# First V load in three pieces, score tiles in another order, and the third batch's projection moved forward, in a fused linear-attention and FFN kernel

## The chip, the cores and the metric

The kernel runs on one core of one Trainium2 chip. The metric is the device time of one execution in microseconds (us). The kernel before takes 512.08 us (median of three runs, 511.97 to 513.61). A ratio is the mean time of one kernel's runs over the mean of the other's of the same rounds on the same chip, so it is not quite the ratio of the medians that are quoted. Below 1 means faster than the kernel before. "Same" is a difference under 2%.

Engine names in the profile: PE is TensorE, DVE is VectorE, ACT is ScalarE, POOL is GpSimd, SP is SyncE. A "q" after the name (SPq) is the engine's instruction queue, here issuing a DMA.

## The reference

Eight batches of eight heads, 1,024 tokens of 64 features. Keys and values are projected from 1,024 tokens to 64 rows, so attention is against 64 projected keys; its result is the input of a two-layer FFN with squared ReLU.

```python
# q, k, v: (8, 8, 1024, 64); E, F: (64, 1024); w_in: (512, 2048); w_out: (2048, 512)
k_proj = np.einsum('ks,bhsd->bhkd', E, k)
v_proj = np.einsum('ks,bhsd->bhkd', F, v)
scores = scale * np.matmul(q, k_proj.transpose(0, 1, 3, 2))
attn = softmax(scores)                                    # cut: max, exp, sum
x = np.matmul(attn, v_proj)                               # cut: to (8192, 512)
h = np.maximum(x @ w_in, 0.0)
return h * h @ w_out                                      # float32 (8192, 512)
```

## The kernel before

TensorE's order is written by hand; the instructions of the other engines and of the DMA queues are ordered by a scheduler when the kernel is built. The FFN of batch b is the backbone. A plan inserts the attention work of batch b+1, and the projections of batch b+2, between numbered steps of that FFN. In what follows, "second batch" is b = 1, "third batch" is b = 2, and so on.

```python
    qkv_pool = ctx.enter_context(tc.tile_pool(name="qkv", bufs=2))   # two K, two V, two Q tiles, 1 MB each
    out_pool = ctx.enter_context(tc.tile_pool(name="outp", bufs=4))  # o_sb: four tiles of 256 KB
    fps = ctx.enter_context(tc.tile_pool(name="fps", bufs=4, space=bass.MemoryType.PSUM))   # "bank"
    # ... cut ...
    def load(t, src):
        return nc.gpsimd.dma_start(t, src)               # all loads: GpSimd's queue

    def load_kvq(b):
        tiles = []
        for name, src in (("K_sb", k), ("V_sb", v), ("Q_sb", q)):
            t = qkv_pool.tile([P, H, NI, D], BF16, name=name)
            tiles.append((t, load(t[:], tokens(src, b))))
        return tiles
    # ... cut: first K, Q loads in halves ...
    for g in range(2):
        load(V0[:, half[g]], tokens(v, 0, h=half[g]))
    # ... cut ...
    W_IN_PIECES = ((0, 2), (2, 4), (4, 8), (8, 12), (12, 16))
    # ... cut: one load a piece, then four w_out loads, the first batch's second Q half before the last ...

    SCORE_QUADS = ((LO, 0, 0, LO), (HI, 0, 1, LO), (LO, 1, 1, HI), (HI, 1, 0, HI))
    VALUE_QUADS = ((LO, 0, 0, LO), (HI, 0, 1, HI), (HI, 1, 1, LO), (LO, 1, 0, HI))

        def transpose_q_dma(self):                       # SyncE's queue: 1 MB, SBUF to SBUF
            nc.sync.dma_start_transpose(
                self.qT[:].rearrange("p h n t -> p (h n) t"), self.Q[:].rearrange("p h i d -> p (h i d)")
            )

        def scores_mm(self, ps, pr, n):                  # four 64x64 tiles of the array
            for o, par, a, r in SCORE_QUADS:
                h = 2 * pr + a
                nc.tensor.matmul(
                    ps[o, par], lhsT=self.kT[r, h % 4, h // 4, :], rhs=self.qT[r, h, n, :], start=True, stop=True
                )
    # ... cut ...
        def store(self, c, tb, ps, m=slice(0, DM)):      # PSUM -> o_sb by ScalarE, then SyncE's queue
            o = out_pool.tile([P, DM], F32, name="o_sb")
            nc.scalar.copy(o[:, m], ps[:, m])
            i = 2 * (2 * c + tb % 2) + tb // 2
            nc.sync.dma_start(out_rows[self.b, i, :, m], o[:, m])
    # ... cut: the plan of batch b ...
                if b + 2 < B:
                    if b == 0:
                        at(61, coming.project)           # reads the third batch's K and V
                        at(63, coming.transpose_q_dma)
                        at(64, coming.transpose_k)
                    else:
                        at(27, coming.project)
                        at(30, coming.transpose_q_dma)
                        at(29, coming.transpose_k_dma)
```

SyncE's queue carries both the 1 MB transposes of Q and the output stores. And a load into a K, V or Q tile can be issued only when the tile's earlier content has been consumed: K and V by the projection on TensorE, Q by its DMA transpose (from the third batch on).

Names in the profile lines: kp and vp are the projected K and V, kT and qT the transposed kp and Q, xT the attention result, hsq the squared hidden layer of the FFN. ps_bank and ps_att are tiles in PSUM, into which the matmuls write; a "bank" is one of the four ps_bank tiles. o_sb is an output tile in SBUF on its way to memory.

The softmax here doesn't subtract the row's maximum and nothing guards it: scores larger than these inputs give would overflow.

## Time and profile before

| quantity | value | view |
|---|---|---|
| time | 512.08 us (511.97 to 513.61) | runs |
| span in the profile | 510.0 us | page |
| TensorE busy | 497.0 us, 97% | page, part 1 |
| TensorE's longest wait for data | 1.4 us, second half of the first V | waits |
| granted clock | 1.000 | cores |
| FFN period of one batch, later batches | 60.43 to 60.49 us | chain |

The page of the kernel before. In part 2 each column is a fortieth of the span (12.75 us) and a digit is the busy share in tenths; PEclk is the granted TensorE clock. The last line is from part 4, the chain of work that ended last, by engine.

```profile
span 510.0 us, 6889 instructions
...
PE 497.0 (97%) x2710; PEld 222.8 (44%) x2761; DVE 216.7 (42%) x437; ACT 272.4 (53%) x411; POOL 32.0 (6%) x44
...
PE   8799999999999999999999999999999999999997
...
PEclk9999999999999999999999999999999999999999
DMA  9999999899996199104931060101102011010102
...
PE 88%; DMA 7%; issue 2%; POOL 1%; ACT 1%; DVE 1%; POOLq 0%; ACTq 0%
```

TensorE bounds this kernel: it is at 9 in every column but the first two and the last. DMA is at 8 or 9 in the first 12 columns, some 150 us. So the early transfers compete with one another, although TensorE's work hides nearly all of it.

From the waits of TensorE in the kernel before (what waited and for what, us in total, times, longest), the ones that the first V and the last weights cause:

```profile
PE ps_bank L204 <- DMA V_sb<-in_v_dram: 1.4, 1, 1.4
...
PE ps_att L266 <- DVE vp L208: 0.5, 1, 0.5
...
PE ps_bank L364 <- DMA w_out_131<-in_moe_w_out_dram: 0.2, 1, 0.2
```

The first two, 1.9 us, are the second V half and the copy of its projection: they are what the first part of the change addresses.

Now the stretch between 90 and 140 us. First the timeline of GpSimd's queue in the kernel before: start, duration of the issue, engine, line, what is loaded, count, and in brackets the idle time before and what ended it.

```profile
91.02 1.75 POOL L76 DMA_DIRECT2D Q_sb<-in_q_dram  x2 [30.16 <-DMA qT<-Q_sb]
111.09 0.87 POOL L76 DMA_DIRECT2D Q_sb<-in_q_dram  x1 [18.32 <-DMA qT<-Q_sb]
111.95 0.88 POOL L76 DMA_DIRECT2D K_sb<-in_k_dram  x1
112.82 1.09 POOL L76 DMA_DIRECT2D V_sb<-in_v_dram  x1
```

The two loads at 91.02 are Q of the fourth and fifth batch. The one at 111.09 is Q of the sixth batch: it waited 18.3 us for a DMA transpose to consume the tile. The fifth batch's K and V stand behind it in the queue and are issued at 111.95 and 112.82, though their tiles had been free since the third batch's projection, which ended at 87.6 in TensorE's timeline, 24 us earlier.

The timeline of SyncE's queue in the kernel before. The long durations are those of DMA transposes: the queue goes on to the next instruction only when more than half of the transpose has been moved (numbers below).

```profile
101.59 6.96 SPq L248 DMA_TRANSPOSE qT<-Q_sb  x1
108.60 5.32 SPq L373 DMA_DIRECT2D out_dram<-o_sb  x6
116.13 21.16 SPq L248 DMA_TRANSPOSE qT<-Q_sb  x1
```

The transpose issued at 101.59 (Q of the fourth batch) holds the queue for 6.96 us; at 108.60 six output stores follow, the first four of them issued one right after the other by 110.24. The o_sb tiles of these four had been filled at 77.06 to 90.37 (ScalarE's copies): their stores stand behind this transpose in the queue's order, and it waits for its Q, which landed at 101.52. The trace says more. At the end of such an issue, 675, 672 and 669 KB of the 1,049 KB had been started in the first three transposes. The three later ones, which begin with no load beside them, hold the queue 4.0 to 4.2 us and let it go at 800, 852 and 594 KB. While 1 KB load packets run beside it, a transpose (256 B packets) moves 39 KB per us and the loads 154; alone it moves 290. Both kinds have about 152 packets in each us, one for one. The Trainium skill ("DMA: Bandwidth & Descriptors", Queues, rings and completion order) says that each DMA engine takes its queue rows in turn, a packet from each; the equal counts of this trace agree with that. (A packet of that page holds several descriptors; whether a packet record of the trace is one of those is not shown.)

The first of the four stores landed at 111.10. What waits for it, in ScalarE's timeline and then in TensorE's, of the kernel before:

```profile
111.17 0.58 ACT L371 COPY o_sb<-ps_bank 128x512 f32<-128x512 f32 x1 [1.12 <-DMA out_dram<-o_sb]
```

```profile
112.78 1.03 PE L364 MATMUL ps_bank<-w_out_124,hsq 128*128 128x512 bf16 x4
```

ScalarE's copy of an output tile to o_sb starts at 111.17, just after the store that freed that o_sb tile; the matmul group of 112.78 writes the PSUM bank which that copy freed. TensorE did not wait; the slack is about 1 us.

The next transpose, issued at 116.13, holds the queue for 21.16 us, to 137.29. Only two output tiles are copied meanwhile (ScalarE at 118.94 and 122.39), so two of the four o_sb tiles stay free, and TensorE waits for nothing there.

### The profile page before, as it was taken

The page shows a single profiled execution, that of the slowest core. Times are in us where ns is not written, and L with a number is a line of the kernel's source. Part 1 is how long each engine was busy: PE and PEld are TensorE (multiplying, and loading weights), DVE is VectorE, ACT ScalarE, POOL GpSimd, SP SyncE. Part 2 cuts the span into 40 slices and gives each one's busy share as a digit, 9 for nine tenths or more (in the row PEclk, how much of TensorE's full clock was granted, in tenths as well). Part 3 has the DMA queues.
Part 4 walks back from the last instruction along what each step waited for, and adds up shares of the span by engine and source line. Part 5 has one row for each costly group of instructions (what it writes and reads, how often), then busy time and mean ns, then how long its engine had stood idle before and what let it go on. Part 6 is the DMA issues. An engine that isn't in the chain of part 4 may idle for free.

```text
span 510.0 us, 6889 instructions
## 1 busy us (share of the span) xinstructions
PE 497.0 (97%) x2710; PEld 222.8 (44%) x2761; DVE 216.7 (42%) x437; ACT 272.4 (53%) x411; POOL 32.0 (6%) x44
## 2 busy tenths in 40 slices
PE   8799999999999999999999999999999999999997
PEld 4344444444444444444444444444444444444444
DVE  2442766444434445235452345444443443522130
ACT  2564484664718556374645736366472755544351
POOL 7320100121000020001000000000000000000000
PEclk9999999999999999999999999999999999999999
DMA  9999999899996199104931060101102011010102
GB/s 156 204 205 222 226 207 202 132 220 207 195 217 125 56 185 201 65 0 126 181 78 42 17 160 1 62 22 42 53 1 82 1 41 42 31 54 21 63 0 82
DMA packets 67840, 53.92 MB, mean 106 GB/s; under 512 B 29152, under 2 KB 59616, under 8 KB 67808
## 3 DMA queue, kind: packets, MB, share of 16 engines
q0 software_dynamic: 30880, 29.49, 36.8%
q1 hardware_dynamic: 36928, 23.99, 17.5%
q8 instruction: 21, 0.34, 0.3%
q14 instruction: 11, 0.09, 0.1%
HBM read 59.24 MB, written 16.78 MB: 149 GB/s over the span
## 4 chain that ended last, share of the span: by engine, by line
PE 88%; DMA 7%; issue 2%; POOL 1%; ACT 1%; DVE 1%; POOLq 0%; ACTq 0%
PE ps_bank L364 41%; PE ps_bank L358 40%; DMA w_out_131<-in_moe_w_out_dram 4%; DMA w_in_116<-in_moe_w_in_dram 3%; PE ps_bank L185 2%; PE ps_att L256 1%; PE ps_att L290 1%; PE ps_att L312 1%; PE ps_bank L312 1%; DVE rs L300 0%; PE ps_bank L241 0%; DVE xT L341 0%; POOL K_sb L76 0%; POOL V_sb L76 0%; ACT expT L270 0%
## 5 line engine op out<-in xcount | busy, mean ns | idle before, releaser
L355 DVE TENSOR_TENSOR hsq<-h_relu 128x512 bf16<-128x512 bf16 x256 | 108.9, 426 | 192.9 <-ACT h_relu L354 192.0
L354 ACT ACTIVATE h_relu<-ps_bank 128x512 bf16<-128x512 f32 x256 | 151.7, 599 | 69.3 <-PE ps_bank L358 69.2
L364 PEld LDWEIGHTS <-hsq 128*128 128x128 bf16 x1040 | 99.5, 98 | 123.6 <-issue 9.3
L371 ACT COPY o_sb<-ps_bank 128x512 f32<-128x512 f32 (+1 forms) x65 | 37.6, 579 | 119.7 <-PE ps_bank L364 110.9
L364 PE MATMUL ps_bank<-w_out_124,hsq 128*128 128x512 bf16 (+1 forms) x257 | 65.6, 376 | 0.2
L364 PE MATMUL ps_bank<-w_out_131,hsq 128*128 128x512 bf16 (+1 forms) x251 | 64.1, 376 | 1.4 <-issue 1.1
L364 PE MATMUL ps_bank<-w_out_128,hsq 128*128 128x512 bf16 (+1 forms) x252 | 64.3, 376 | 1.1 <-issue 1.0
L364 PE MATMUL ps_bank<-w_out_126,hsq 128*128 128x512 bf16 (+1 forms) x249 | 64.2, 376 | 1.1 <-issue 0.8
L300 DVE COPY rs<-rs 32x1024 f32<-32x1024 f32 x60 | 41.3, 689 | 47.2 <-ACT rs L295 45.8
L358 PE MATMUL ps_bank<-xT,w_in_122 128*128 128x512 bf16 x255 | 58.9, 380 | 0.0
L358 PE MATMUL ps_bank<-xT,w_in_118 128*128 128x512 bf16 x250 | 57.7, 380 | 0.4
L358 PE MATMUL ps_bank<-xT,w_in_120 128*128 128x512 bf16 x247 | 57.4, 379 | 0.4
L270 ACT ACTIVATE expT<-ps_att 128x1024 bf16<-128x1024 f32 x32 | 31.8, 1024 | 18.1 <-PE ps_att L256 18.1
L358 PEld LDWEIGHTS <-w_in_120 128*128 128x128 bf16 x256 | 24.9, 98 | 30.4 <-issue 0.4
L358 PEld LDWEIGHTS <-w_in_118 128*128 128x128 bf16 x256 | 24.9, 98 | 30.2 <-issue 0.4
L358 PEld LDWEIGHTS <-w_in_122 128*128 128x128 bf16 x256 | 24.4, 98 | 31.1 <-issue 2.7
L358 PE MATMUL ps_bank<-xT,w_in_114 128*128 128x512 bf16 x128 | 30.6, 379 | 0.3 <-DVE xT L341 0.2
L358 PE MATMUL ps_bank<-xT,w_in_116 128*128 128x512 bf16 x126 | 30.0, 379 | 0.1
L294 ACT ACTIVATE rs<-ps_att 128x1024 f32<-128x1024 f32 x15 | 15.3, 1023 | 12.7 <-PE ps_att L290 12.7
L316 DVE TENSOR_TENSOR xT<-ps_att,rs 128x512 bf16<-128x512 f32 x28 | 18.1, 686 | 8.7 <-PE ps_att L312 8.4
L358 PEld LDWEIGHTS <-w_in_114 128*128 128x128 bf16 x128 | 12.4, 98 | 15.6 <-issue 1.3
L358 PEld LDWEIGHTS <-w_in_116 128*128 128x128 bf16 x128 | 12.5, 98 | 15.2 <-issue 0.2
(71 smaller groups left out, 233.9 us busy)
## 6 DMA issues: line engine op xcount, KB each, us to landing
out_dram<-o_sb SPq DMA_DIRECT2D x63, 256.0 KB, 2.0
K_sb<-in_k_dram POOLq DMA_DIRECT2D x7, 1024.0 KB, 22.1
V_sb<-in_v_dram POOLq DMA_DIRECT2D x7, 1024.0 KB, 26.7
Q_sb<-in_q_dram POOLq DMA_DIRECT2D x7, 1024.0 KB, 15.0
K_sb<-in_k_dram POOLq DMA_DIRECT2D x2, 512.0 KB, 7.1
V_sb<-in_v_dram POOLq DMA_DIRECT2D x2, 512.0 KB, 12.0
Q_sb<-in_q_dram POOLq DMA_DIRECT2D x2, 256.0 KB, 7.6
w_in_118<-in_moe_w_in_dram POOLq DMA_DIRECT2D x1, 512.0 KB, 15.5
```

The source lines that it names most:

```text
L185: nc.tensor.matmul(ps[LO, :], lhsT=ET[:, i, :], rhs=self.K[:, :, i, :], start=f, stop=l)
L256: nc.tensor.matmul(ps[o, par], lhsT=self.kT[r, h % 4, h // 4, :], rhs=self.qT[r, h, n, :], start=True, stop=True)
L270: nc.scalar.activation(e[:], ps[:], AF.Exp, scale=SCALE)
L294: nc.scalar.activation(rs[1][:], ps[:], AF.Ln)
L300: nc.vector.tensor_copy(rs[j][lack:lack + 32], rs[j][have:have + 32])
L312: nc.tensor.matmul(ps_x[par][o], lhsT=self.vp[r, 2 * pr + a, :], rhs=e[r, par], start=True, stop=True)
L316: nc.vector.tensor_tensor(out=self.xT[:, pr, :, par], in0=ps_x[par].rearrange("p (c t) -> p c t", c=2), in1=rs[:, par].rearrange("p (c t) ...
L354: nc.scalar.activation(r[:], ps[:], AF.Relu)
L355: nc.vector.tensor_tensor(out=self.hsq[c][:, fb, :], in0=r[:], in1=r[:], op=ALU.mult)
L358: nc.tensor.matmul(ps[:], lhsT=w_in_blk(cb, fb), rhs=self.xT[:, cb, c].rearrange("p a t -> p (a t)"), start=(cb == 0), stop=(cb == NCB - 1),)
L364: nc.tensor.matmul(ps[:, m], lhsT=self.hsq[c][:, fb, tb * P:(tb + 1) * P], rhs=w_out_blk(fb)[:, m], start=(fb == 0), stop=(fb == NFB - 1),)
L371: nc.scalar.copy(o[:, m], ps[:, m])
```

## The change

It has three parts with separate intents.

1. V of the first batch comes in three pieces instead of two, behind a small w_in piece, so that the first FFN matmuls can fill the waits for V. The third w_in piece becomes two.
2. The four score matmuls of a group are issued by alternating row halves of the array, so that weight loads can overlap the matmul before.
3. The third batch's projection moves from step 61 to step 51, into a block of attention work, where the array already works in tiles of 64 columns; the transposition of kp goes to step 57.

```diff
@@ loads of the first V
-    for g in range(2):
-        load(V0[:, half[g]], tokens(v, 0, h=half[g]))
+    V_PIECES = (slice(0, 4), slice(4, 6), slice(6, 8))
+    load(V0[:, V_PIECES[0]], tokens(v, 0, h=V_PIECES[0]))
@@
-    W_IN_PIECES = ((0, 2), (2, 4), (4, 8), (8, 12), (12, 16))
+    W_IN_PIECES = ((0, 2), (2, 4), (4, 6), (6, 8), (8, 12), (12, 16))
-    for lo, hi in W_IN_PIECES:
+    for j, (lo, hi) in enumerate(W_IN_PIECES):
         t = wpool.tile([P, NCB, (hi - lo) * P], BF16, name=f"w_in_{lo}")
         load(t[:], w_in_view[:, :, lo * P:hi * P])
         for fb in range(lo, hi):
             w_in_at[fb] = (t, fb - lo)
+        if j == 0:
+            for h in V_PIECES[1:]:
+                load(V0[:, h], tokens(v, 0, h=h))
@@ scores
-    SCORE_QUADS = ((LO, 0, 0, LO), (HI, 0, 1, LO), (LO, 1, 1, HI), (HI, 1, 0, HI))
+    SCORE_QUADS = ((LO, 0, 0, LO), (LO, 1, 1, HI), (HI, 0, 1, LO), (HI, 1, 0, HI))
@@ cut: project_v by a slice of heads; chunk_values by pairs; the first four FFN blocks
@@ interleaved by input quarter; a warm-up matmul
@@ plan of the first batch
+                at(1, att.project_v, V_PIECES[1])
+                at(2, att.chunk_values, 0, 1, (0,))
+                at(2, att.project_v, V_PIECES[2])
+                at(3, att.chunk_values, 0, 1, (1,))
@@
                     if b == 0:
-                        at(61, coming.project)
+                        at(51, coming.project)
                         at(63, coming.transpose_q_dma)
-                        at(64, coming.transpose_k)
+                        at(57, coming.transpose_k)
```

The diff does not show one thing that the built program does: with the third batch's K and V consumed earlier in TensorE's order, the scheduler, which decides when the kernel is built, orders GpSimd's queue otherwise. Before, it holds Q of the fourth, fifth and sixth batch, then K and V of the fifth. After, it holds Q of the fourth and fifth, then K and V of the fifth, and then Q of the sixth.

More of the change, by code (lines that the diff above doesn't have):

```diff
@@ L197, in project_k, with project_v @@
             self.keep_k(ps[LO, 0:C // 2], g, nc.scalar.copy if g == 0 else None)
-        def project_v(self, g):
-            ps = bank()
+        def project_v(self, h):
+            n = (h.stop - h.start) * D
+            ps = att_psum()[:, 0, 0:n]
             for i in range(NI):
@@ L204, in project_v @@
                     nc.tensor.matmul(
-                        ps[o, 0:C // 2], lhsT=FT[:, i, :], rhs=V0[:, half[g], i, :],
-                        start=(i == 0), stop=(i == NI - 1),
+                        ps[o], lhsT=FT[:, i, :], rhs=V0[:, h, i, :], start=(i == 0), stop=(i == NI - 1)
                     )
-            nc.vector.tensor_copy(self.vp[:, half[g]], ps[:, 0:C // 2].rearrange("k (h d) -> k h d", d=D))
+            nc.vector.tensor_copy(self.vp[:, h], ps.rearrange("k (h d) -> k h d", d=D))
         def transpose_k(self, gs=(0, 1)):
@@ L331, in chunk_sums, with chunk_values @@
             self.rs[g] = self.inverse(ps)
-        def chunk_values(self, c, g):
+        def chunk_values(self, c, g, pairs=(0, 1)):
             ps = att_psum()
-            e, rs = self.e.pop(g), self.rs.pop(g)
-            for j in range(2):
+            e, rs = self.e[g], self.rs[g]
+            for j in pairs:
                 s = slice(j * HC, (j + 1) * HC)
                 self.values_mm(ps[:, :, s], 2 * g + j, e[:, :, s])
-            for j in range(2):
+            for j in pairs:
                 s = slice(j * HC, (j + 1) * HC)
@@ L380, in steps @@
                 if first:
-                    banks = [bank() for _ in range(2)]
-                    for g in range(2):
-                        for fb in range(2):
-                            for cb in (2 * g, 2 * g + 1):
+                    banks = [bank() for _ in range(4)]
+                    for part in (
+                        ((0, (0, 1)),), ((1, (0, 1)),), ((2, (0, 1)),),
+                        ((0, (2, 3)), (1, (2, 3)), (2, (2, 3)), (3, (0, 1, 2, 3))),
+                    ):
+                        for cb, fbs in part:
+                            for fb in fbs:
                                 self.first_mm(c, fb, cb, banks[fb])
-                            if g == 1:
-                                self.square(c, fb, banks[fb])
+                                if cb == NCB - 1:
+                                    self.square(c, fb, banks[fb])
                         yield
-                    fb0 = 2
+                    fb0 = 4
                 for fb in range(fb0, NFB):
@@ L448 @@
         warm(2)
-        att.project_v(0)
+        att.project_v(V_PIECES[0])
         warm(1)
@@ L452 @@
         att.chunk_values(0, 0)
-        warm(1)
-        att.project_v(1)
-        att.chunk_values(0, 1)
+        warm(2)
         coming = None
```

## The prediction

> **What bounds it now.** TensorE: the page shows PE busy 497.0 of 510.0 us, and the chain that ended last is 88% PE. In the wait view TensorE waits for data only early: 1.4 us for the second V half (landed 19.69), 0.5 us for its vp copy, 0.2 us for xT, 0.2 us for the last w_out piece (landed 42.31, used 42.35). Early loads are bandwidth-bound: 512 KB land every 2.55 us until 42 us.
>
> **Part 1, V in pieces.** It fills these waits with the first FFN matmuls. From the timeline I estimate TensorE 1.2 us further on at the third w_in piece (24.4 instead of 25.6). But the bytes ahead of the second Q half (39.76) and the last w_out piece are the same, so TensorE waits there and resumes at about 42.4 instead of 42.35. Net 0 to +0.1 us.
>
> **Part 2, score order.** The four 64x64 matmuls of a group already start within 9 ns (102.575 to 102.584) and groups follow after 0.24 us, as do the value matmuls, which alternate already. Net 0. The Trainium skill ("TensorE: Matmul & The Clock Gate", Part 3) says weight loads overlap matmuls only when the row group differs; this trace shows nothing to gain.
>
> **Part 3, the third batch's projection.** In the attention block it saves one entry and exit of column tiling, about 0.1 us; transposing kp right behind a tile's eviction costs about 0.3 us. The larger effect is indirect: the order on GpSimd's DMA queue changes. Before, the fifth batch's K and V loads stand behind a Q load that waits for the fourth batch's DMA transpose (issued 111.95 and 112.82). After, they stand before it, issued at about 93 us directly behind two Q loads. So 2 MB more are in flight during that transpose (issued 101.59, landed 110.56).
>
> What that does: beside loads, transposes move 39 KB/us and loads 154 (120 to 141 us); alone they move 290. SyncE's queue stays blocked until about 670 KB of the 1049 have moved (three transposes: 675, 672, 669). About 2.2 MB of loads remain at 104.5: 14.4 us, so the queue frees at about 119.7 instead of 108.55. Behind it stand four stores holding all four o_sb buffers; the first lands 2.5 us later, about 122.2 (before 111.10). The ScalarE eviction that needs that buffer (111.17 before) starts there, and TensorE's third output tile of the second batch, which reuses its PSUM bank (started 112.78, 1 us of slack), starts at about 123. That is a 10 us stall on the critical path; later work only shifts. Then the clock is cold: the first eight warm-up matmuls took 3.59 us instead of 1.73; I add 1.7 us.
>
> **Sum.** 512.1 + 0.2 + 10 + 1.7 = 524.0 us; range 516 to 527. Faster by over 2%: 0.03; within 2%: 0.31; slower: 0.66.
>
> **What would show it.** V_sb and vp waits gone, larger waits for Q_sb and w_out near 39 to 42 us. Score groups still 0.24 us. K and V issued near 93 us; the second long transpose holding SyncE's queue about 18 us; a ScalarE wait for an out store of about 11 us; a TensorE gap near 113 to 123 us, then matmuls twice as far apart for 3 us. Batch period after that 60.45 us, as before.
>
> **What would make it wrong.** If the transpose's share of the DMA engines is larger, or the loads are issued later, the stall shrinks or vanishes and the time is 511.5 to 513. If the clock stays up, 522. If the last weights land sooner, part 1 keeps up to 1.2 us.

## The result, and the profile after

| kernel | median us | range | runs | ratio (95% interval) |
|---|---|---|---|---|
| before, same rounds | 512.75 | 511.97 to 513.61 | 5 | |
| after | 526.35 | 525.39 to 527.82 | 5 | 1.0271 (1.0250 to 1.0293) |

The changed kernel is slower by 2.7%, 13.6 us at the medians. The page of the profile after, the same lines:

```profile
span 525.2 us, 6923 instructions
...
PE 500.9 (95%) x2727; PEld 224.8 (43%) x2778; DVE 216.4 (41%) x438; ACT 272.5 (52%) x411; POOL 33.2 (6%) x46
...
PE   7999999964999999999999999999999999999997
...
PEclk8999999995999999999999999999999999999999
DMA  9999999999998049810881024010201011010102
```

One place stands out: columns 9 and 10 (counted from 1, so 105 to 131 us), where PE drops to 6 and 4, and PEclk to 5 in the second of them. Everything after it is as full as before. PE's busy time went up by 3.9 us; the other 11.3 of the 15.2 us of span are idle time.

TensorE's waits after. The group of V waits is gone, and one new wait is as long as nearly the whole loss:

```profile
PE ps_bank L367 <- ACT o_sb L374: 12.0, 1, 12.0
...
PE ps_bank L218 <- ACT o_sb L374: 0.3, 1, 0.3
```

The timeline of GpSimd's queue after: K and V of the fifth batch are issued directly behind the two Q loads, 17.5 us earlier than before.

```profile
92.71 1.75 POOL L76 DMA_DIRECT2D Q_sb<-in_q_dram  x2 [30.96 <-DMA qT<-Q_sb]
94.44 0.90 POOL L76 DMA_DIRECT2D K_sb<-in_k_dram  x1
95.31 0.90 POOL L76 DMA_DIRECT2D V_sb<-in_v_dram  x1
125.08 0.88 POOL L76 DMA_DIRECT2D Q_sb<-in_q_dram  x1 [28.87 <-DMA qT<-Q_sb]
```

SyncE's queue after, in the same window as before:

```profile
103.13 18.77 SPq L251 DMA_TRANSPOSE qT<-Q_sb  x1
121.95 5.62 SPq L376 DMA_DIRECT2D out_dram<-o_sb  x6
```

The transpose issued at 103.13 holds the queue for 18.77 us instead of 6.96, because 2,825 KB of loads moved beside it, against 666 KB before. The first store is issued at 121.95 instead of 108.60. ScalarE and TensorE after:

```profile
125.20 0.59 ACT L374 COPY o_sb<-ps_bank 128x512 f32<-128x512 f32 x1 [14.26 <-DMA out_dram<-o_sb]
```

```profile
108.70 5.13 PE L367 MATMUL ps_bank<-w_out,hsq 128*128 128x512 bf16 x23 [0.16 <-issue]
125.83 5.00 PE L367 MATMUL ps_bank<-w_out,hsq 128*128 128x512 bf16 x12 [12.01 <-ACT o_sb L374]
```

All four o_sb tiles are held by stores that stand behind the transpose, so ScalarE's copy waits 14.26 us, until the first store lands. TensorE waits 12.01 us for the bank that this copy frees. Its next twelve matmuls take 5.00 us (the group of 23 before them took 5.13), which is the halved clock. The chain of work of the profile after says the same in its own way, with start, duration and what ran:

```profile
108.70 5.14 PE ps_bank L367 x23
113.84 8.06 SPq L251
...
121.95 3.17 DMA out_dram<-o_sb
...
125.20 0.59 ACT o_sb L374
...
125.83 4.43 PE ps_bank L367 x10
```

Read downwards it is: TensorE's matmuls, then 8.06 us of SyncE's queue held by the transpose, then a store, then ScalarE's copy, then TensorE again. Before, the chain in this stretch was TensorE's alone.

The Trainium skill ("TensorE: Matmul & The Clock Gate", Part 1) says that the clock falls to half after an idle window of about 3.4 us and comes back after about as much busy time. This trace agrees in size: TensorE stops at 113.83, and the record of the granted clock stands at half from 116.76 to 130.41 us (13.65 us, four times 3.413). So it falls 2.9 us after the last matmul and is back 4.6 us after the next one, at 125.83. The matmuls behind the gap start 427 ns apart instead of 216. Eleven of them cost 11 x 0.211 = 2.3 us.

### The profile page after: what moved, and what is told of

It is laid out like the page before. It is cut to its first block, busy times and chain, and to the rows that moved or that the text cites. A ratio compares the mean times of both kernels' runs of the same rounds, so it can differ in the third digit from the quotient of the medians. Undisturbed runs are those within 1.5% of the kernel's fastest.

```text
span 525.2 us, 6923 instructions
## 1 busy us (share of the span) xinstructions
PE 500.9 (95%) x2727; PEld 224.8 (43%) x2778; DVE 216.4 (41%) x438; ACT 272.5 (52%) x411; POOL 33.2 (6%) x46
## 4 chain that ended last, share of the span: by engine, by line
PE 92%; DMA 2%; issue 2%; SPq 2%; ACT 1%; DVE 1%; ACTq 0%; DVEq 0%; POOLq 0%
PE ps_bank L361 42%; PE ps_bank L367 40%; PE ps_bank L188 2%; SPq L251 2%; PE ps_att L259 1%; DMA K_sb<-in_k_dram 1%; PE ps_att L293 1%; PE ps_att L315 1%; PE ps_bank L315 1%; DVE xT L344 1%; DMA out_dram<-o_sb 1%; PE ps_bank L197 1%; PE ps_bank L148 1%; PE ps_bank L234 0%; ACT o_sb L374 0%
## 5 line engine op out<-in xcount | busy, mean ns | idle before, releaser
L367 PE MATMUL ps_bank<-w_out,hsq 128*128 128x512 bf16 (+1 forms) x1009 | 225.7, 378 | 15.4 <-ACT o_sb L374 12.0
L361 PE MATMUL ps_bank<-xT,w_in 128*128 128x512 bf16 x1006 | 225.2, 379 | 1.7 <-DVE xT L344 0.6
L361 PEld LDWEIGHTS <-w_in 128*128 128x128 bf16 x1024 | 99.2, 98 | 122.6 <-issue 5.1
L297 ACT ACTIVATE rs<-ps_att 128x1024 f32<-128x1024 f32 x15 | 15.4, 1024 | 11.9 <-PE ps_att L293 11.8
L319 DVE TENSOR_TENSOR xT<-ps_bank,rs 128x512 bf16<-128x512 f32 x28 | 18.5, 685 | 0.8
L299 ACT ACTIVATE rs<-rs 128x1024 f32<-128x1024 f32 x15 | 16.0, 1067 | 0.2
L298 ACT ACTIVATE rs<-rs 128x1024 f32<-128x1024 f32 x15 | 15.9, 1058 | 0.3
L76 POOL DMA_DIRECT2D Q_sb<-in_q_dram x10 | 8.6, 863 | 92.6 <-DMA qT<-Q_sb 83.5
L188 PE MATMUL ps_bank<-K_sb,ET 128*64 128x512 bf16 x56 | 13.4, 382 | 0.0
L189 PE MATMUL ps_bank<-V_sb,FT 128*64 128x512 bf16 x56 | 13.4, 382 | 0.0
L259 PE MATMUL ps_att<-qT,kT 64*64 64x512 bf16 (+1 forms) x144 | 11.2, 359 | 0.2 <-DVE kT L222 0.2
L148 PE MATMUL ps_bank<-zeros 128*128 128x512 bf16 x24 | 8.5, 462 | 1.4 <-DVE zeros L103 1.2
```

The lines of the kernel that those rows point to most:

```text
L188: nc.tensor.matmul(ps[LO, :], lhsT=ET[:, i, :], rhs=self.K[:, :, i, :], start=f, stop=l)
L259: nc.tensor.matmul(ps[o, par], lhsT=self.kT[r, h % 4, h // 4, :], rhs=self.qT[r, h, n, :], start=True, stop=True)
L299: nc.scalar.activation(rs[1][:], rs[1][:], AF.Exp, scale=-1.0)
L319: nc.vector.tensor_tensor(out=self.xT[:, pr, :, par], in0=ps_x[par].rearrange("p (c t) -> p c t", c=2), in1=rs[:, par].rearrange("p (c t) ...
L361: nc.tensor.matmul(ps[:], lhsT=w_in_blk(cb, fb), rhs=self.xT[:, cb, c].rearrange("p a t -> p (a t)"), start=(cb == 0), stop=(cb == NCB - 1),)
L367: nc.tensor.matmul(ps[:, m], lhsT=self.hsq[c][:, fb, tb * P:(tb + 1) * P], rhs=w_out_blk(fb)[:, m], start=(fb == 0), stop=(fb == NFB - 1),)
```

## The experiments

The theory: nearly the whole loss comes from the order of loads on GpSimd's queue, which part 3 changed by way of the scheduler. More loads run beside a DMA transpose, the transpose holds SyncE's queue longer, the stores stand behind it, o_sb runs out, ScalarE's copy waits, a PSUM bank stays taken, TensorE waits. The rivals: (a) the new TensorE order of part 3 is slow by itself; (b) part 1 or 2 costs something; (c) more DMA traffic slows TensorE some other way than through o_sb; (d) the clock falls for a reason of its own, and the wait follows. (In the expectations "rival A" is (b) and "rival B" is (a).) Two rounds of runs were made, with nine runs of the kernel before in each: median 511.99 us (511.37 to 512.72) in the first and 512.38 (511.30 to 513.10) in the second. The first round held e1 to e4, the second e5 to e7.

### Parts 1 and 2 without part 3 (e1)

The changed kernel with part 3's lines put back:

```diff
-                        at(51, coming.project)
+                        at(61, coming.project)
                         at(63, coming.transpose_q_dma)
-                        at(57, coming.transpose_k)
+                        at(64, coming.transpose_k)
```

> The change without its third part: V in pieces and the new score order, the third batch's projection where it was. The order of loads on GpSimd's queue stays that of before. My theory (the loss comes from the order of loads, which only part 3 changes): within 0.3% of before, 511.5 to 514 us; no TensorE wait for an o_sb eviction. Rival A (cutting V and w_in costs it, by more or smaller DMAs or the longer prologue): most of the 13.6 us stays, about 525 us.

Measured: 512.05 us (511.87 to 513.20, five runs), ratio 1.0008 (0.9995 to 1.0021). No wait for o_sb. So parts 1 and 2 neither gain nor cost; rival (b) falls. Where part 1's gain goes is seen in TensorE's timeline of this run (start, duration, group, wait before it):

```profile
18.44 0.59 PE L361 MATMUL ps_bank<-xT,w_in 128*128 128x512 bf16 x2 [0.34 <-DVE xT L344]
...
35.12 4.48 PE L367 MATMUL ps_bank<-w_out,hsq 128*128 128x512 bf16 x20
40.03 1.07 PE L234 MATMUL ps_bank<-ident,Q_sb 128*128 128x128 bf16 x16 [0.43 <-DMA Q_sb<-in_q_dram]
...
42.55 1.02 PE L367 MATMUL ps_bank<-w_out,hsq 128*128 128x512 bf16 x4 [0.59 <-DMA w_out<-in_moe_w_out_dram]
```

The first FFN matmul starts at 18.44, against 21.67 in the kernel before. Some of that head start is only another order of the same work; where both kernels reach the same point, the start of the second layer, the lead in this pair of traces is 0.8 us (35.12 against 35.93). It is not shown to come from part 1: over all profiled runs this start lies at 34.70 to 36.70 us in the four without part 1 (before, e2, e4, e6) and at 35.12 to 36.79 in the five with it. Then TensorE waits 0.43 us for the second Q half and 0.59 us for the last w_out piece, and goes on at 42.55, where the kernel before went on at 42.35. The last weights landed at 42.51 here and 42.31 before (42.06 to 42.63 in the traces without part 1, 42.16 to 42.71 in those with it): the bytes in front of them are the same, whatever their order.

For part 2, one line of TensorE's timeline from the kernel before and one from the changed kernel, each of two score groups (eight matmuls):

```profile
102.58 0.63 PE L256 MATMUL ps_att<-qT,kT 64*64 64x512 bf16 x8
```

```profile
103.46 0.63 PE L259 MATMUL ps_att<-qT,kT 64*64 64x512 bf16 x8
```

0.63 us both times. The Trainium skill ("TensorE: Matmul & The Clock Gate", Part 3) says that weight loads overlap matmuls in flight only when the row group differs. In this trace there was nothing left to overlap: the four matmuls of a group start 2 to 4 ns apart under either order, and the next group 0.24 us after the first. Part 2 was not run alone; that it is worth nothing rests on these lines and on e1.

### Part 3 alone (e2)

```diff
-                        at(61, coming.project)
+                        at(51, coming.project)
                         at(63, coming.transpose_q_dma)
-                        at(64, coming.transpose_k)
+                        at(57, coming.transpose_k)
```

> Before with only the third batch's projection and kp transpose moved to steps 51 and 57. My theory: all of the loss, 524 to 527 us, with the fifth batch's K and V loads issued near 93 us, the second long transpose holding SyncE's queue 18 to 19 us, and one TensorE wait of about 12 us for the o_sb eviction. Rival A: as before, 512 us. Rival B (the projection's new place in TensorE's order costs it, not the loads): also 525 us, so this run doesn't tell B apart.

Measured: 524.25 us (523.31 to 524.73, four runs), ratio 1.0238 (1.0223 to 1.0253). TensorE waits 9.2 us for o_sb (about 12 were expected); the second transpose holds SyncE's queue from 100.94 to 119.53. Part 3 carries the loss, but this does not yet say by which way: it changes TensorE's order and the load order together.

### The changed kernel with the old load order (e3)

Q of the sixth batch is put before K and V of the fifth on GpSimd's queue. The order of instructions on TensorE, VectorE, ScalarE and SyncE in the built program is that of the changed kernel.

```diff
                 if b + 2 < B:
@@ cut: load_kvq becomes load_kv, load_q and load take its place
-                    coming = Attention(b + 2)
-                    coming.load()
+                    coming, early_q = Attention(b + 2), None
+                    if b == 2:
+                        coming.load_q()
+                        later = Attention(b + 3)
+                        early_q = later.load_q()
+                    elif b == 3:
+                        coming = later
+                    coming.load(early_q)          # K and V, issued after early_q where it is given
+                    if b not in (2, 3):
+                        coming.load_q()
```

> The whole change, with one thing undone: the sixth batch's Q load, which waits for the fourth batch's transpose, stands before the fifth batch's K and V loads again, as it did before. TensorE, VectorE, ScalarE and SyncE have exactly the changed kernel's instruction order. My theory: the stall goes, SyncE's queue is held about 7 us, time 511 to 514 us. Rival A and rival B: still 524 to 527 us.

Measured: 512.64 us (512.39 to 513.43, five runs), ratio 1.0016 (1.0002 to 1.0030). One wait view line of TensorE, and the transpose in SyncE's timeline of this run:

```profile
PE ps_bank L369 <- ACT o_sb L382: 1.1, 1, 1.1
```

```profile
102.65 6.87 SPq L259 DMA_TRANSPOSE qT<-Q_sb  x1
```

All of part 3's TensorE order is there, and the loss is gone. The wait of 1.1 us for o_sb is not the one in question: it ends at 154.87 us, and ScalarE's copy there waited for a store (issued 142.57, landed 154.15) that stood behind later transposes. At the studied place TensorE's 36 matmuls from 107.81 on run without a gap. Rival (a) falls.

### The kernel before with the new load order (e4)

The other direction: only the sixth batch's Q load is issued after the fifth batch's V load. All other orders are those of the kernel before.

```diff
-    def load_kvq(b):
+    def load_kvq(b, after=None):
         ...
-            tiles.append((t, load(t[:], tokens(src, b))))
+            if name == "Q_sb" and after is not None:
+                with tc.issue_after(after.ins):
+                    tiles.append((t, load(t[:], tokens(src, b))))
+            else:
+                tiles.append((t, load(t[:], tokens(src, b))))
@@ cut: load passes "after" on
-                    coming.load()
+                    last = coming.load(last if b == 3 else None)   # returns its V load
```

> The kernel before, with one thing done: the fifth batch's K and V loads stand before the sixth batch's Q load. All other engines keep before's order. My theory: the loss appears without any of the three parts: K and V issued near 93 us, SyncE's queue held about 18 us, TensorE idle about 12 us from 113 us, 524 to 527 us. Rivals A and B: as before, 512 us.

Measured: 524.17 us (523.79 to 524.88, four runs), ratio 1.0241 (1.0227 to 1.0255). TensorE's wait and the transpose on SyncE's queue in this run:

```profile
PE ps_bank L369 <- ACT o_sb L376: 10.5, 1, 10.5
```

```profile
101.03 18.80 SPq L253 DMA_TRANSPOSE qT<-Q_sb  x1
```

One reordered load, with no TensorE instruction moved, costs 12 us. The step of the prediction is measured here nearly by itself: the queue is free at 119.83 (predicted 119.7), and TensorE's stall is 10.5 us (predicted 10). That these are so close is partly luck: the transpose started 0.6 us earlier than in the kernel before (101.03 against 101.59) and held the queue 0.7 us longer than the 18.1 us of the prediction.

### The changed kernel with eight o_sb tiles (e5)

```diff
-    out_pool = ctx.enter_context(tc.tile_pool(name="outp", bufs=4))
+    out_pool = ctx.enter_context(tc.tile_pool(name="outp", bufs=8))
```

> The whole change with eight o_sb buffers in place of four; order on every engine as in the changed kernel, loads included. My theory says the chain to TensorE passes through the o_sb buffers: the long transpose still holds SyncE's queue 18 to 19 us and still lands near 122 to 125 us, but no eviction waits for a store there, the TensorE gap goes, and the time is 511.5 to 513.5 us. A rival that the slow transpose hurts TensorE by another way (scores waiting for qT, or contention of the loads): 522 to 527 us.

Measured: 512.39 us (511.93 to 512.76, five runs), ratio 1.0004 (0.9991 to 1.0016). The transpose and the copies of ScalarE in this run:

```profile
103.36 19.93 SPq L251 DMA_TRANSPOSE qT<-Q_sb  x1
```

```profile
110.72 0.59 ACT L374 COPY o_sb<-ps_bank 128x512 f32<-128x512 f32 x1
```

The transpose holds SyncE's queue even longer (19.93 us), and the loads compete as in the changed kernel. But ScalarE's copy runs at 110.72, because a tile is free, and TensorE has no such wait. So the loss reaches TensorE only through o_sb: rival (c) falls. Rival (d) falls as well: the granted clock in this run is 1.000, so it was the gap that made TensorE cold. This run also bounds the direct effect of all three parts together without the stall: 1.0004, or 0.2 us, the interval being -0.5 to +0.8 us.

### Half the dose (e6)

If the bytes beside the transpose set the time that it holds the queue, then one 1 MB load instead of two must give about half the loss. In the kernel before, only K of the fifth batch is put before Q of the sixth; V comes after it.

```diff
+    def load_one(name, src, b, after=None): ...
-        def load(self):
-            (self.K, first), (self.V, _), (self.Q, _) = load_kvq(self.b)
-            return first
+        def load(self, later=None):
+            self.K, last = load_one("K_sb", k, self.b)
+            if later is not None:
+                self.Q, _ = load_one("Q_sb", q, self.b)
+                later.Q, last = load_one("Q_sb", q, later.b, last)
+            self.V, _ = load_one("V_sb", v, self.b, last if later is not None else None)
+            if self.Q is None:
+                self.Q, _ = load_one("Q_sb", q, self.b)
@@ cut: the plan calls coming.load(later) for b = 2
```

> The kernel before with half of the dose: only the fifth batch's K load (1 MB) stands before the sixth batch's Q load, its V load after it. If the stall is the time that extra bytes share the engines with the transpose: 1.2 MB instead of 2.2 MB are left when the transpose starts, 7.7 us at 154 KB/us, SyncE's queue held until about 114 us, TensorE idle 4 to 5 us; with 0 to 2.3 us for the clock 516 to 519 us. If any change of the order costs the same (a rival: the wait of the reordered loads themselves), about 524 us.

Measured: 518.61 us (517.90 to 519.21, four runs), ratio 1.0125 (1.0109 to 1.0142). By the 2% rule this counts as "same", but the interval is clear of 1, and it is about half of e4's loss, as expected.

```profile
PE ps_bank L369 <- ACT o_sb L376: 4.3, 1, 4.3
```

```profile
101.59 12.64 SPq L253 DMA_TRANSPOSE qT<-Q_sb  x1
```

From the trace, for the second long transpose (Q of the fourth batch) of each profiled run; "loads beside it" are the bytes that the load queue moved between its issue and its landing:

| kernel | loads beside it, KB | it holds SyncE's queue, us | TensorE waits for o_sb, us | span, us |
|---|---|---|---|---|
| before | 666 | 6.96 | none | 510.0 |
| e1, parts 1 and 2 | 724 | 6.87 | none | 510.1 |
| e3, after with old load order | 733 | 6.87 | none (1.1 later, see e3) | 511.4 |
| e6, before with K early | 1,738 | 12.64 | 4.3 | 516.2 |
| e4, before with K and V early | 2,828 | 18.80 | 10.5 | 522.6 |
| e2, part 3 alone | 2,851 | 18.59 | 9.2 | 522.1 |
| e7, after again | 2,827 | 18.55 | 11.3 | 524.1 |
| after | 2,825 | 18.77 | 12.0 | 525.2 |
| e5, after with eight o_sb | 2,796 | 19.93 | none | 510.6 |

Each further 1,000 KB of loads hold the queue 5.3 to 5.7 us longer (before to e6, e6 to e4). In these two, TensorE's wait is 1.3 to 1.4 us less than the hold added over the kernel before: 1.0 us of it is the slack, the rest are small shifts (in e6 TensorE reaches this point 0.5 us later, in e4 the transpose starts 0.6 us earlier). The cold clock comes on top.

### The changed kernel again (e7)

The changed kernel, unaltered, beside e5 and e6, because the first result stood 2 us above e2 and e4.

> The changed kernel again, beside the others on one chip, to see whether its 2 us over part 3 alone is steady. With part 3 alone the long wait was 9.2 us in the profile, here 12.0. If steady: 525.5 to 527 us and the first long transpose landing near 92 us instead of 90.3; if it was the chip: about 524.5 us.

Measured: 525.81 us (525.67 to 526.28, four runs), ratio 1.0268 (1.0252 to 1.0284). So the further 1.5 us over e2 and e4 came again, though they are 0.3% and the intervals of the ratios touch. A difference is seen in the traces: in the four traces that have the changed kernel's whole TensorE order (after, e3, e5, e7) the first long transpose lands at 91.98 to 92.29 us; in the other five (before, e1, e2, e4, e6) at 90.16 to 90.69. The next loads, the next transpose and thus the stores follow that much later; but TensorE, too, comes to the stall later (at 113.45 in e7 against 112.70 in e4). In all nine traces the last 256 B packet of that transpose ends at 89.7 to 90.3 us; the landing follows 0.4 to 0.5 us later in five of them and 2.0 us later in the four. In those four, a 16.4 KB instruction-fetch packet of 1.20 us starts at 89.7 to 90.1 us, beside the last packets; in the others it starts at 90.55 or later. That goes with the delay in every trace, but no run moved the fetch, so the cause of this 1.5 us stays open.

No version here beats the kernel before; e1, e3 and e5 are the same as it. With TensorE busy 497 of 510 us, there was not much to win. (Some matmul records are missing in that trace; the one of e5, with 2,778 weight loads and as many matmuls, shows 503.9 of 510.6 us.)

## Why the prediction was right

- **The outcome.** Predicted 524.0 us, 516 to 527; measured 526.35. Slower, as the larger chance said.
- **Load order to queue hold.** Predicted: K and V issued near 93 us, the transpose holding SyncE's queue about 18 us, to 119.7. Measured 94.44 and 95.31, and 18.77 us, to 121.90; in e4, which has the kernel before around it, 92.62 and 93.49, and 18.80 us, to 119.83. What was assumed, that the queue is released when about 670 KB have moved, held for this transpose in every profile (672 to 681 KB); it does not hold for the later transposes without loads beside them (see the profile before). e3 and e4 show that the load order is the cause.
- **Queue hold to TensorE.** Predicted by the way of the stores, the four o_sb tiles, ScalarE's copy and the PSUM bank, with a stall of 10 us; measured 12.0 and 11.3 in the changed kernel, 10.5 in e4, 9.2 in e2. e5 shows that the way is this one and no other. The stall of the changed kernel is up to 2 us longer than the term said. In the profile after, its second transpose starts 1.5 us later than the prediction had it (103.13 against 101.59) and holds the queue 0.7 us longer, and the first store takes 3.2 us in place of 2.5; against this, TensorE itself comes to the stall 1.0 us later (113.83 against 112.78). The late start was not foreseen, and its cause is open (see e7).
- **Cold clock.** Predicted 1.7 us; measured about 2.3 us. The estimate took the start-up's eight matmuls; here eleven ran at half speed.
- **Part 1.** Predicted a lead of 1.2 us, given back at the last weights. That nothing is won is right (e1: 1.0008). The lead itself is not shown: the 0.8 us of e1 at the second layer lie within the spread of the traces without part 1 (34.70 to 36.70 us). The sign that the prediction named, longer waits for Q_sb and w_out near 40 us, is in e1's profile (0.4 and 0.6 us), but also in that of e4, which has no part 1 (0.4 and 0.6 us). It is not in that of the changed kernel, where TensorE itself came later (first FFN matmul at 20.51; it had waited 1.1 us for K, and ran one window of 3.4 us at half clock at the start).
- **Part 2.** Predicted nothing; two score groups take 0.63 us before and after.
- **Part 3's direct costs.** Predicted 0.3 us for kp's transposition right behind an eviction; the profile after shows a wait of 0.3 us there (L218). The 0.1 us predicted to be saved is too small for these runs; e5's 1.0004 is the bound on all of it.

Of the 2.4 us between 524.0 and 526.35, some 0.7 are the base: the kernel before of the same rounds took 512.75 us, and the sum starts from 512.1. The loss itself was predicted as 11.9 us and measured as 13.6. Of its terms, the stall (12.0 or 11.3 in place of 10) and the clock (2.3 in place of 1.7) were a little small, together by 1.9 to 2.6 us in the two profiled executions, which covers the 1.7 us that were missing.

## What to carry to other kernels

When an edit moves the consumer of an operand, look at which loads a scheduler then puts earlier and what they collide with: here a queue shared by a long DMA transpose and the output stores turned 2 MB of well-meant prefetch into a 12 us TensorE stall. Read the order of every queue in the built program and not only the diff, and cost the chain from transfer to queue, to buffer, to PSUM bank, with rates from the trace. Ask also what stands behind the held queue at that moment: the hold of 21.16 us in the kernel before cost nothing. If such a chain has to be cut, more output buffers (e5) or the old load order (e3) each did it alone. Putting the stores ahead of the transpose in SyncE's queue was not tried.

## What the Trainium skill lacked or had wrong

- How long a DMA transpose holds its issuing queue: no page gives a figure. "Perfetto Trace Analysis" (Summary: the profiler window per engine type) puts the data movement of a DMA issued through hardware descriptor generation outside the window that the profiler shows; its timeline of such a DMA lets the movement begin inside the window, without a size. Here the issue of a 1 MB transpose lasts 6.87 to 19.93 us for the transpose studied, and ends when 672 to 681 of its 1,049 KB have been started; so under load most of the movement lies inside the window.
- The rate of a transpose beside other traffic: "DMA: Bandwidth & Descriptors" (Latency and other measured facts) gives 261 GB/s, or 350 to 400 in the contiguous case. Here one alone moved 290 KB per us (290 GB/s), but beside 1 KB load packets only 39 KB per us against the loads' 154. The page's rule of turns between queue rows (Queues, rings and completion order) fits it, at about 152 packets each per us, but no page draws the conclusion that small transpose packets get a fifth of the bytes.
- Instruction fetches: "Runtime: NRT & Kernel Launch" (Instruction fetch mechanics) is the page for them, but it gives no duration. Here a 16.4 KB fetch packet took 0.9 to 2.0 us (1.20 us in the four late traces of e7). Whether it delays the landing of a transpose is open.
